# Eight normalised-row buffers shared with the gate tiles, earlier weight halves and a new engine order in a fused attention and feed-forward kernel

## The chip, the cores and the metric

The kernel runs on one core of one Trainium2 chip. The metric is the device time of one execution in microseconds (us). A profiled execution has a span about 2.0 us shorter than its time.

An execution more than 1.5% above the fastest of the same kernel counts as slow and is left out of the ratios.

TensorE is PE, VectorE DVE, ScalarE ACT and GpSimd POOL.

## The reference, cut to what matters

```python
x  = A_x                                   # [1, 2048, 512] bf16
xn = layernorm(x)
q, k, v = split(xn @ wqkv)                 # 32 heads of 16
# each row looks at 8 rows behind it, 2 apart (row, row-2, ... row-14)
logits = einsum(q, k[window]) * scale      # softmax over the 8
s = (softmax(logits) . v[window]) @ wo
h = gelu(xn_in @ w_gate) * (xn_in @ w_up)  # xn_in = xn, 1792 columns
return x + s * silu(h @ w_down)
```

## The kernel before

The 2048 rows are worked on in four blocks of 512, a block being four tiles of 128 rows. Each tile is normalised on DVE into an `xn` buffer and then turned, so that its columns lie along partitions. PE turns the tiles of blocks 0 and 1; a DMA transpose turns those of blocks 2 and 3 (tiles 8 to 15) and frees the `xn` buffer when it has landed. There are four such buffers.

```python
def norm(t, dep):
    def fn():
        tiles["xn", t] = lnpool.tile([P, D], BF16, name="xn_t")    # ring of G["lnb"] = 4
        nc.vector.tensor_scalar(out=tiles["xn", t][:], in0=x_sb[:, t, :], ...)
...
def turned(t, dep):
    def fn():
        nc.sync.dma_start_transpose(out=xnT[:, :, t * P : (t + 1) * P], in_=tiles["xn", t][:])
```

v goes to DRAM and comes back in overlapping windows, by gathers with many short rows. GpSimd and the sync engine issue those of block 0 as soon as v of block 0 is stored, at about 26 us:

```python
def load_values(j, half):
    ...
    a = add("pool", ..., lambda: fn(nc.gpsimd, (0, 1)), deps=[v_stored[j]], ...)
    b = add("sp", 1.0, lambda: fn(nc.sync, (2, 3)), deps=[v_stored[j], ...], ...)
```

The scores of a block are elementwise products of q and shifted k on DVE, pairwise sums (`res`), and a reduction over the head's columns on PE (`L_ps`). Before the first transpose PE runs nine matmuls on zeros, `warm_up(9, TQ)`. A small scheduler in the kernel takes estimated durations (the table `G`) and emits the instructions in the order it finds; on the chip each engine keeps that order.

The softmax here doesn't subtract the row's maximum and nothing guards it: scores larger than these inputs give would overflow.

## Time and profile before

| | kernel before |
|---|---|
| time, three runs | 225.7 us median (225.19 to 225.85) |
| time of the profiled execution | 228.5 us (span 226.6) |
| PE busy | 219.9 us, 97% |
| DVE busy | 185.4 us, 82% |

### The profile page before, as it was taken

How to read it: one execution, taken by the hardware profiler on the slowest of the kernel's cores; microseconds unless marked ns; L12 is line 12 of the kernel's file. 1: busy time of each engine (PE TensorE's matmuls, PEld its weight loads, DVE VectorE, ACT ScalarE, POOL GpSimd, SP SyncE). 2: the span in 40 equal slices, each digit the busy share in tenths (PEclk: the TensorE clock that was granted, in tenths of full speed). 3: DMA queues.
4: the chain of work that ended last, by engine and by line, in shares of the span. 5: the costliest groups of instructions: out<-in, count | busy, mean ns of one | idle time of the engine just before them, and what ended most of it. 6: DMA issues, size and time to landing. Idle time of an engine off the chain costs nothing.

```text
span 226.6 us, 3230 instructions
## 1 busy us (share of the span) xinstructions
PE 219.9 (97%) x1195; PEld 105.4 (47%) x1195; DVE 185.4 (82%) x271; ACT 139.7 (62%) x223; POOL 14.8 (7%) x46
## 2 busy tenths in 40 slices
PE   7999999979999999999999999999999999999994
PEld 2897544534544444444444444444444444444443
DVE  4699979999999999999999989999995997122132
ACT  3368787785778735187986524789735186777211
POOL 7100210000000120000022000002020000000000
PEclk9999999999999999999999999999999999999999
DMA  6935899966960843010062710001662100000001
GB/s 211 360 129 153 205 240 175 227 192 186 337 242 2 188 113 94 30 48 0 3 157 45 175 49 25 23 0 35 157 154 57 48 24 0 0 0 3 23 23 46
DMA packets 23567, 23.68 MB, mean 105 GB/s; under 512 B 5872, under 2 KB 22528, under 8 KB 23552
## 3 DMA queue, kind: packets, MB, share of 16 engines
q1 hardware_dynamic: 17184, 12.75, 22.7%
q10 hardware_dynamic: 5056, 6.46, 9.2%
q0 software_dynamic: 1312, 4.28, 8.3%
q8 instruction: 9, 0.15, 0.3%
q14 instruction: 6, 0.05, 0.1%
HBM read 18.22 MB, written 4.21 MB: 99 GB/s over the span
## 4 chain that ended last, share of the span: by engine, by line
PE 74%; DVE 12%; DMA 5%; ACT 5%; issue 1%; ACTq 0%; DVEq 0%
PE y_ps L818 22%; PE g_ps L756 18%; PE u_ps L756 17%; PE qkv_ps L449 9%; PE s_ps L806 6%; DMA xnT<-xn_t 3%; DVE stats L317 3%; DVE res L561 3%; DVE prod L589 2%; PE O_ps L723 2%; DVE xn_t L338 2%; DMA wo_sb<-in_A_wo_dram 1%; ACT L766 1%; DMA x_sb<-in_A_x_dram 1%; ACT gl L766 1%
## 5 line engine op out<-in xcount | busy, mean ns | idle before, releaser
L756 PE MATMUL g_ps<-xnT,wg_sb 128*128 128x512 bf16 x224 | 57.5, 379 | 0.2
L756 PE MATMUL u_ps<-xnT,wu_sb 128*128 128x512 bf16 x224 | 57.6, 379 | 0.0
L818 PE MATMUL y_ps<-wd_sb,hT 128*128 128x512 bf16 (+2 forms) x238 | 51.5, 367 | 0.0
L449 PE MATMUL qkv_ps<-xnT,wqkv_sb 128*128 128x512 bf16 (+2 forms) x256 | 45.0, 338 | 0.3 <-ACT vst L473 0.2
L766 ACT ACTIVATE gl<-g_ps 128x512 bf16<-128x512 f32 x56 | 33.5, 599 | 11.5 <-PE g_ps L756 10.3
L561 DVE TENSOR_TENSOR res<-prod 128x2048 bf16<-128x2048 bf16 x32 | 39.1, 1221 | 0.5
L777 ACT ACTIVATE hT<-u_ps 128x512 bf16<-128x512 f32 x56 | 33.5, 598 | 9.3 <-PE u_ps L756 9.1
L701 DVE TENSOR_TENSOR prod<-attn,v_arr 128x2048 bf16<-128x2048 bf16 x32 | 38.8, 1219 | 0.0
L589 DVE TENSOR_TENSOR prod<-q_sb,k_sb 128x2048 bf16<-128x2048 bf16 x32 | 38.4, 1218 | 0.0
L818 PEld LDWEIGHTS <-hT 128*128 128x128 bf16 x238 | 22.5, 98 | 26.5 <-issue 1.3
L781 DVE TENSOR_TENSOR hT<-gl,hT 128x512 bf16<-128x512 bf16 x56 | 23.3, 421 | 14.1 <-ACT hT L777 14.0
L449 PEld LDWEIGHTS <-wqkv_sb 128*128 128x128 bf16 x256 | 27.1, 113 | 15.9 <-issue 0.9
L756 PEld LDWEIGHTS <-wg_sb 128*128 128x128 bf16 x224 | 21.7, 98 | 27.4 <-issue 1.9
L756 PEld LDWEIGHTS <-wu_sb 128*128 128x128 bf16 x224 | 21.1, 98 | 26.3 <-issue 2.1
L830 ACT ACTIVATE sil<-y_ps 128x512 bf16<-128x512 f32 (+2 forms) x17 | 9.7, 572 | 34.1 <-PE y_ps L818 34.0
L835 DVE TENSOR_TENSOR sg<-sil,s_ps 128x512 bf16<-128x512 bf16 (+2 forms) x17 | 11.1, 654 | 14.4 <-PE s_ps L806 7.6
L521 POOL DMA_DIRECT2D v_arr<-vT_dram x16 | 9.3, 586 | 150.4 <-DVE prod L701 130.3
L806 PE MATMUL s_ps<-wo_sb,o_sb 128*128 128x512 bf16 (+2 forms) x68 | 16.6, 366 | 0.0
L734 ACT ACTIVATE o_sb<-O_ps 128x1024 bf16<-128x1024 f32 x8 | 8.2, 1023 | 9.0 <-PE O_ps L723 9.0
L462 ACT ACTIVATE q_sb<-qkv_ps 128x512 bf16<-128x512 f32 x16 | 9.6, 599 | 5.5 <-PE qkv_ps L449 5.5
L473 ACT ACTIVATE vst<-qkv_ps 128x512 bf16<-128x512 f32 x16 | 9.1, 597 | 5.7 <-DMA wo_sb<-in_A_wo_dram 2.7
L317 DVE BATCH_NORM_STATS2 stats<-x_sb 128x6 f32<-128x512 bf16 x16 | 10.8, 672 | 2.2 <-DMA x_sb<-in_A_x_dram 2.2
(54 smaller groups left out, 114.7 us busy)
## 6 DMA issues: line engine op xcount, KB each, us to landing
v_arr<-vT_dram POOLq DMA_DIRECT2D x16, 260.0 KB, 5.8
v_arr<-vT_dram SPq DMA_DIRECT2D x16, 260.0 KB, 5.6
vT_dram<-vst SPq DMA_DIRECT2D x16, 128.0 KB, 5.6
out_dram<-sg SPq DMA_DIRECT2D x15, 128.0 KB, 1.7
wu_sb<-in_B_w_up_dram ACTq DMA_DIRECT2D x2, 896.0 KB, 7.1
wg_sb<-in_B_w_gate_dram ACTq DMA_DIRECT2D x2, 896.0 KB, 5.2
wd_sb<-in_B_w_down_dram ACTq DMA_DIRECT2D x1, 1792.0 KB, 11.9
wqkv_sb<-in_A_wqkv_dram SPq DMA_DIRECT2D x2, 512.0 KB, 6.0
```

Of the source, the lines that this page charges most:

```text
L317: nc.vector.bn_stats(out=stats[:, t, :], in_=x_sb[:, t, :])
L449: nc.tensor.matmul(ps[:, i * n : (i + 1) * n], lhsT=wqkv_sb[:, which, ws], rhs=xnT[:, dk, j * TQ + lo : j * TQ + lo + n], start=(dk == 0), ...
L561: nc.vector.tensor_tensor(out=res[:], in0=a[:], in1=b[:], op=ALU.add)
L589: nc.vector.tensor_tensor(out=prod[:], in0=tiles["q", j][:, c, :].unsqueeze(1).to_broadcast([P, 4, TQ]), in1=kwin, op=ALU.mult,)
L701: nc.vector.tensor_tensor(out=prod[:], in0=tiles["attn", j][:, w2, :].unsqueeze(1).to_broadcast([P, 4, TQ]), in1=tiles["va", j, half][:, 4 ...
L756: nc.tensor.matmul(ps[:], lhsT=w[:, dk, fc * P : (fc + 1) * P], rhs=xnT[:, dk, j * TQ : (j + 1) * TQ], start=(dk == 0), stop=(dk == NC - 1),)
L766: nc.scalar.activation(out=tiles["gl", j, fc][:], in_=tiles["g_ps", j, fc][:], func=AF.Gelu_apprx_tanh)
L777: nc.scalar.activation(out=hidden(), in_=tiles["u_ps", j, fc][:], func=AF.Copy)
L781: nc.vector.tensor_tensor(out=h, in0=tiles["gl", j, fc][:], in1=h, op=ALU.mult)
L806: nc.tensor.matmul(tiles["s", t, cs.start][:], lhsT=tiles["o", j][:, c, tt * P : (tt + 1) * P], rhs=wo_sb[:, c, cs], start=(c == 0), stop= ...
L818: nc.tensor.matmul(tiles["y", t, cs.start][:], lhsT=tiles["h", j, fc // (NF // 2)][:, fc % (NF // 2), tt * P : (tt + 1) * P], rhs=wd_sb[:, ...
L835: nc.vector.tensor_tensor(out=tiles["sg", t][:, cs], in0=tiles["sil", t][:, cs], in1=tiles["s", t, cs.start][:], op=ALU.mult,)
```

## The change

The intent is to take the wait for a free `xn` buffer off DVE's way to the first scores. The ring gets eight buffers, and its memory is found by letting the output tiles' silu and gate buffers use the same ring later. The first halves of `w_gate` and `w_up` are loaded earlier, and the order of all engines is found anew from a changed table of durations. Core of the diff, with cuts:

```diff
-    ... xturn=3.702, lnb=4, ... TRACT=((1, 1),), trig=[1, 6, 3, 5], ...
+    ... xturn=4.638, lnb=8, ... TRACT=((1, 1),), trig=[0, 0, 5, 6], ... wd_at=2, ...
...
-    fpool = pool("fpool", 3)
...
-                tiles["xn", t] = lnpool.tile([P, D], BF16, name="xn_t")
+                tiles["xn", t] = lnpool.tile([P, D], BF16, name="xn_t", tag="xn")
...
-                tiles["sil", t] = fpool.tile([P, D], BF16, name="sil")
-                tiles["sg", t] = fpool.tile([P, D], BF16, name="sg")
+                tiles["sil", t] = lnpool.tile([P, D], BF16, name="sil", tag="xn")
+                tiles["sg", t] = lnpool.tile([P, D], BF16, name="sg", tag="xn")
```

(The scheduler's bookkeeping of the ring follows; it is left out here.)

More of the change, by code (lines that the diff above doesn't have):

```diff
@@ L25 @@
 G = dict(
-    MM=0.215, COL8=0.564, COL16=1.157, TR=0.24, PROD=1.197, HMUL2=0.34, STATS=0.766, NORM=0.323,
-    TRCOPY=0.465, ACT1=0.56, ACT2=0.963, TABLE=1.08, HOP=0.248, LOOK=0.046, xturn=3.702, lnb=4,
-    tcol=384, vst=2.785, vload=10.575, vissue=2.707, x2=15.772, x3=17.887, FULL=(0, 1, 2, 3),
-    BETWEEN={1: 6}, NPE=2, TRACT=((1, 1),), trig=[1, 6, 3, 5], s_prio=[1.0, 2.0, 3.5, 4.25],
-    v_prio=[2.0, 2.0, 3.0, 3.5], e_lat=0.796, b_lat=1.188, l_lat=0.1, o_lat=1.013, t_lat=0.381,
-    s_lat=0.105, smode=[2, 2, 2, 0], p_sum=-0.4, p_red=-0.5, p_tr=-1.0, p_h=-1.4, wo_at=0, wd_at=0,
-    fb=4, ab=2, ob=1, prb=3, rsb=4, vab=2, x_early=[3.2, 3.5, 3.8, 4.1],
+    MM=0.214, COL8=0.3, COL16=1.6, TR=0.2, PROD=1.142, HMUL2=0.34, STATS=0.755, NORM=0.328,
+    TRCOPY=0.39, ACT1=0.543, ACT2=0.811, TABLE=1.35, HOP=0.17, LOOK=0, xturn=4.638, lnb=8, tcol=384,
+    vst=2.974, vload=6.199, vissue=3.668, x2=12.258, x3=15.244, FULL=(0, 1, 2, 3), BETWEEN={1: 6},
+    NPE=2, TRACT=((1, 1),), trig=[0, 0, 5, 6], s_prio=[1.0, 3.5, 5.0, 5.0], v_prio=[2.75, 1.75, 3.0,
+    3.0], e_lat=0.291, b_lat=1.428, l_lat=0.468, o_lat=0.81, t_lat=0.496, s_lat=1.042, smode=[2, 2,
+    1, 2], p_sum=-0.4, p_red=-0.5, p_tr=-0.45, p_h=-2.0, wo_at=0, wd_at=2, fb=4, ab=2, ob=1, prb=3,
+    rsb=4, vab=2, x_early=[3.2, 3.5, 3.8, 4.1],
 )
@@ L87, in ready @@
             return None
-        for ring, key in t.takes:
-            n = len(self.taken[ring]) - self.bufs[ring]
+        for i, (ring, key) in enumerate(t.takes):
+            n = len(self.taken[ring]) - self.bufs[ring] + sum(r == ring for r, _ in t.takes[:i])
             if n >= 0:
@@ L185 @@
     order = Order(
-        {"xn": G["lnb"], "q": 3, "vst": 4, "va": G["vab"], "pr": G["prb"], "res": G["rsb"], "attn": 2, "o": 2, "h0": 1, "h1": 1, "gl": 3, "sg": 3,
+        {"xn": G["lnb"], "q": 3, "vst": 4, "va": G["vab"], "pr": G["prb"], "res": G["rsb"], "attn": 2, "o": 2, "h0": 1, "h1": 1, "gl": 3,
          "f": G["fb"], "a": G["ab"], "O": G["ob"]}
@@ L879, in finish @@
                     "act", ACT1, lambda cs=cs: silu(cs), deps=[ym], prio=-0.5, func="silu",
-                    takes=[("sg", t)] if cs.start == 0 else [], frees=[("f", ("y", t, cs.start))],
+                    takes=[("xn", ("sil", t)), ("xn", ("sg", t))] if cs.start == 0 else [], frees=[("f", ("y", t, cs.start))],
                 )
@@ L883, in finish @@
                     "dve", 0.06 + 0.62 * part(cs), lambda cs=cs: gate(cs), deps=[a, sm], prio=-1.8,
-                    frees=[("f", ("s", t, cs.start))],
+                    frees=[("f", ("s", t, cs.start))] + ([("xn", ("sil", t))] if end else []),
                 )
@@ L890, in finish @@
                 st = add("act" if split and end else "sp", 0.6, lambda cs=cs: store(cs), deps=[d], prio=-0.5)
-                add(("dma", "out", t, cs.start), 2.0, lambda: None, deps=[(st, 0.0)], frees=[("sg", t)] if end else [])
+                add(("dma", "out", t, cs.start), 2.0, lambda: None, deps=[(st, 0.0)], frees=[("xn", ("sg", t))] if end else [])
         def in_turn():
```

## The prediction

> **What bounds the kernel now.** I read the page first, then the chain of waits, then the table of who waited for whom, then the timelines of TensorE (PE) and VectorE (DVE). The page gives the engine shares.
>
> ```profile
> span 226.6 us, 3230 instructions
> PE 219.9 (97%) x1195; PEld 105.4 (47%) x1195; DVE 185.4 (82%) x271; ACT 139.7 (62%) x223; POOL 14.8 (7%) x46
> PE 74%; DVE 12%; DMA 5%; ACT 5%; issue 1%; ACTq 0%; DVEq 0%
> ```
>
> PE is the engine that everything ends behind. Busy time alone does not prove it, because matmuls are pipelined and overlap in the record, so I took starts, not durations. In the timeline a group of four 128x512 matmuls starts every 0.86 us (30.91, 31.77, 32.64), that is 216 ns each, and it does so almost without a break from 18.8 us to the last matmul at 223 us. So I looked for every place where the next group starts late. These are the lines, with what stands before and after them.
>
> ```profile
> 45.68 0.40 PE L614 MATMUL L_ps<-res,quad 128*32 128x512 bf16 x4
> 47.36 0.40 PE L614 MATMUL L_ps<-res,quad 128*32 128x512 bf16 x4 [1.28 <-DVE res L561]
> 47.69 5.37 PE L449 MATMUL qkv_ps<-xnT,wqkv_sb 128*128 128x512 bf16 x24
> ...
> 53.22 1.04 PE L449 MATMUL qkv_ps<-xnT,wqkv_sb 128*128 128x512 bf16 x4
> 54.45 1.89 PE L449 MATMUL qkv_ps<-xnT,wqkv_sb 128*128 128x512 bf16 x8 [0.19 <-ACT vst L473]
> ...
> 65.12 0.84 PE L614 MATMUL L_ps<-res,quad 128*32 128x512 bf16 x8
> 65.89 1.04 PE L756 MATMUL g_ps<-xnT,wg_sb 128*128 128x512 bf16 x4
> ...
> 111.04 1.04 PE L756 MATMUL u_ps<-xnT,wu_sb 128*128 128x512 bf16 x4
> 112.19 1.02 PE L756 MATMUL g_ps<-xnT,wg_sb 128*128 128x512 bf16 x4
> ```
>
> The reader should see how little there is. An undisturbed score reduction occupies 0.55 us of PE (the one at 106.71 is followed at 107.26); block 0's takes from 45.68 to 47.69, so 1.46 us are lost. Block 1's takes 0.77, so 0.22 lost. At 53.22 four matmuls should take 0.86 and take 1.23: 0.37 lost. At 111.04 they take 1.15: 0.29 lost, and the same once more at 153.54. Sum: 1.46 + 0.22 + 0.37 + 0.29 + 0.29 = 2.63 us. Outside the start (first transposes at 5.66) and the tail (last matmul at 223.3, end at 226.6), that is all PE waits for.
>
> Where the 1.46 us come from is on DVE, and one step further on the DMA queue:
>
> ```profile
> 31.02 0.41 DVE L338 TENSOR_SCALAR xn_t<-x_sb,mv,rstd 128x512 bf16<-128x512 bf16 x1 [0.26 <-DMA xnT<-xn_t]
> 34.42 0.41 DVE L338 TENSOR_SCALAR xn_t<-x_sb,mv,rstd 128x512 bf16<-128x512 bf16 x1 [1.85 <-DMA xnT<-xn_t]
> 46.08 1.22 DVE L561 TENSOR_TENSOR res<-res 128x2048 bf16<-128x2048 bf16 x1
> ```
>
> Four xn buffers hold the normalised rows until the DMA transpose has read them. The last rows of blocks 2 and 3 wait for that transpose (0.26 + 1.85 = 2.11 us of idle DVE), DVE runs without a pause from there to the res at 46.08, and PE waits for its end at 47.3. One of the transposes landed 7.3 us after its issue; they share those microseconds with w_gate's first half (issued 24.21, landed 29.65) and the first gathers of v.
>
> **What the Trainium skill says.** "TensorE: Matmul & The Clock Gate", section "Back-to-back issue gap", gives N/2.4 + 2.5 ns for a warm matmul, 216 ns at N = 512; this trace has 216. So there is nothing to win inside the matmuls. "Perfetto Trace Analysis", section "Identifying the Most-Contended Engine", warns that matmul busy share is no measure of the roofline; here too the 379 ns mean of a matmul record is far from its 216 ns of spacing, hence my use of starts. "DMA: Bandwidth & Descriptors", section "Issuing engines are not separate DMA queues", says transfers started from different engines share the same 16 DMA engines; the trace agrees: w_down (issued 53.15) took 11.9 us to land and the v stores issued beside it 7.3 to 9.5, against about 2 us alone. "ScalarE: Activation LUTs", section "What ACT_TABLE_LOAD costs", states about 1283 ns a load; the trace has 1283.
>
> **The change part by part.** The number of matmuls on PE is the same and their forms are the same (compared in the instruction order of the built kernel), so only waits and positions can move the time.
>
> Eight xn buffers: all eight normalised tiles of blocks 2 and 3 now stand before the first score product, so the 2.11 us of DVE idle go away. The cost is memory alone, paid by giving the silu and gate tiles the same ring; there are 16 output tiles of two buffers each, so four tiles in flight instead of three. That ring isn't needed by the norms any more when the first output tile comes (about 85 us).
>
> Order at the start: ScalarE (ACT) now does the square root of tile 2 before the first evacuation of q, which removes DVE waits of 0.71 and 0.27 us. But the copy of tile 3 stands behind PE's transpose at about 12.5, with only 1.6 us of statistics to fill the time from 10.2, so about 1.1 us come back as a new DVE wait. Zero in sum. Then I add DVE's start spacings from the trace in the new order: statistics 0.80 a tile, norm 0.33, product 1.14, sum behind its own product 1.25, gate multiply 0.34. From the second pair of norms of block 1 (about 18.2): three tiles of statistics, two pairs of norms, four tiles of statistics, two pairs of norms = 27.1. First half of the scores: 4 products and 3 sums, 8.3 us, 35.4. Second half with six gate multiplies: 10.2 us, 45.6. PE arrives at the reduction's second half at about 46.2. So the 1.46 us go, with about 0.5 us to spare.
>
> From there DVE needs 18.2 us to the end of block 1's scores (47.3 to 65.5 in the trace, with the same list of instructions after the change), so 63.8; PE without its stops needs 17.4, from 46.2 to 63.6. DVE is the bound of this stretch by 0.1 to 0.3 us; of the 0.22 us at block 1 about nothing is saved in itself, but both come 1.6 us earlier.
>
> The 0.37 us at 53.2: ACT issues wo in four pieces and w_down in one, 50.51 to 53.8, before it evacuates v. After the change w_down stands behind block 3's evacuations, 0.6 us fewer here: the stop goes or falls under 0.1.
>
> The exponentials of block 2: today between two gelus, two extra table loads and one of the 0.29 stops. Now behind the last evacuation of block 1's feed-forward, ahead of the silus: PE has 14 matmuls (3.0 us) to run before it needs the result, while ACT needs about 0.7 + 1.28 + 1.02 = 3.0 from PE's start of the reduction, which itself takes 0.55. One 0.29 gone; the one of block 3 keeps its pattern and stays.
>
> New waits: the transposes of tiles 6 and 7 now stand one group of eight matmuls later (19.2), with only 0.88 us of matmuls between them and the first q matmul of block 1, which needs both copies on ACT (two of 0.5 behind a latency of 0.4): about 0.2 us lost.
>
> Weights: first halves issued at 13 instead of 18.6 and 24.2. The second half of w_gate goes from 44.9 to about 56.6; PE needs it at about 66. In that place w_up's half took 9.1 us beside w_down; w_down now comes only at about 64, so 5 to 6 us, landed by 63. w_down itself: 1.8 MB at twice the 4.9 us of a lone 0.9 MB half is under 10 us, landed by 74, needed at about 79. Both fit.
>
> Sum: 1.46 + 0.37 + 0.29 gained = 2.12, less 0.2 (new copy wait), less about 0.2 (DVE-bound stretch to block 1) = 1.7. Adding DVE spacings on through blocks 1 to 3 in the new order, each reduction is ready 0.1 to 1.4 us before PE comes to it, the tightest at the first and last value blocks; I take off another 0.2 for those. Net gain 1.5 us: 225.7 - 1.5 = 224.2.
>
> **The rivals.** First: the score chain stays the bound. My 45.6 for DVE has an error of half a microsecond, and any ACT square root that falls behind an evacuation adds to it. Then the wait at the reduction stays at 0.3 to 0.8 and passes whole into block 1: 225.0 to 225.4. For it: the chain of waits runs through DVE statistics and norms from 12 to 26 us. Second: the early weights steal from x. For it: 1.8 MB are issued while the last x tiles land (13.88). Against: x tile 8 is first read at about 15.7, tile 12 after 22, so 2 us to 8 us of slack. It would make 225.5. Third: a late w_gate half or w_down stops PE for one to three microseconds: 226 to 228. For it: transfers of 9.1 and 11.9 us in this trace; against: they were slow because they ran together, and now don't. Fourth: all waits go, PE runs to its floor: 225.7 - 2.6 = 223.1. Nothing in the profile allows less, since the start and the tail have the same instructions.
>
> **Range and chances.** Between the fourth rival and the first lie 223.1 and 225.4, so 223.0 to 225.5 eight times in ten. Faster by over 2% would need under 221.2, 1.9 us below the floor: 0.02. Slower by over 2% would need a new stop of over 4.5 us, which only the third rival at its worst gives: 0.02.
>
> **What would show it.** Right: no wait of the xn norm for the transpose; PE's reduction of block 0 in under 0.8 us; a stop under 0.1 at the v evacuation; the feed-forward pairs of block 0 resuming at 64.0 to 64.5 instead of 65.89; the last matmul at about 221.8. Wrong: the reduction still waits for res (first rival), a gate or down matmul waits for a weight DMA (third), or new breaks of over 0.3 us at a value reduction.

## The result, and the profile after

| | before | after |
|---|---|---|
| time, four runs each | 225.65 us median (225.19 to 225.85) | 225.03 us median (224.88 to 225.28) |
| ratio of fast runs | | 0.9977, 95% from 0.9959 to 0.9994 |

A ratio here is the mean time of one kernel's fast runs over that of the other's of the same rounds, so not quite the ratio of the medians. The time was in the range. The gain was 0.5 us by the ratio (0.0023 of 225.65), not 1.5.

The page of the changed kernel, shares of the span and the chain that ended last:

```profile
span 222.8 us, 3236 instructions
PE 217.1 (97%) x1195; PEld 103.2 (46%) x1195; DVE 185.2 (83%) x271; ACT 138.9 (62%) x222; POOL 14.8 (7%) x46
PE 68%; DVE 26%; ACT 2%; DMA 1%; issue 1%; DVEq 0%
```

The span is 3.8 us shorter than in the profile before, although the times differ by 0.6 at the median. The DMA share of the chain fell from 5% to 1%, DVE's rose from 12% to 26%. PE's timeline of the changed kernel (start, duration, engine, line, operation, count) shows the places that the prediction named:

```profile
43.86 0.61 PE L613 MATMUL L_ps<-res,quad 128*32 128x512 bf16 x8
44.41 4.51 PE L448 MATMUL qkv_ps<-xnT,wqkv_sb 128*128 128x512 bf16 x20
...
61.49 0.40 PE L613 MATMUL L_ps<-res,quad 128*32 128x512 bf16 x4
62.09 0.40 PE L613 MATMUL L_ps<-res,quad 128*32 128x512 bf16 x4 [0.20 <-DVE res L560]
62.42 1.04 PE L755 MATMUL g_ps<-xnT,wg_sb 128*128 128x512 bf16 x4
...
148.06 1.04 PE L755 MATMUL u_ps<-xnT,wu_sb 128*128 128x512 bf16 x4
149.22 1.02 PE L755 MATMUL g_ps<-xnT,wg_sb 128*128 128x512 bf16 x4
```

Block 0's reduction takes 0.55 us from start to the next start, so nothing is lost there. Block 1's takes 0.93, so 0.37 is lost. At 148.06 four matmuls take 1.16 instead of 0.86; by the starts of the single matmuls 0.28 is lost there. One more stop of 0.24 us lies at 18.39, where q of block 1 waits for the copies of tiles 6 and 7.

So far all of this fits the prediction, and by it the time should have fallen by 1.5 us or more. That it did not pointed to the other side of the comparison, the profile of before.

### The profile page after: what moved, and what is told of

The parts are those of the page before. It is cut to its first block, busy times and chain, and to the rows that moved or that the text cites. A ratio compares the mean times of both kernels' runs of the same rounds, so it can differ in the third digit from the quotient of the medians.

```text
span 222.8 us, 3236 instructions
## 1 busy us (share of the span) xinstructions
PE 217.1 (97%) x1195; PEld 103.2 (46%) x1195; DVE 185.2 (83%) x271; ACT 138.9 (62%) x222; POOL 14.8 (7%) x46
## 4 chain that ended last, share of the span: by engine, by line
PE 68%; DVE 26%; ACT 2%; DMA 1%; issue 1%; DVEq 0%
PE y_ps L817 22%; PE g_ps L755 19%; PE u_ps L755 18%; DVE prod L588 8%; DVE res L560 6%; PE s_ps L805 6%; DVE stats L316 4%; DVE xn_t L337 3%; PE O_ps L722 2%; DVE mv L317 1%; DMA x_sb<-in_A_x_dram 1%; DVE hT L780 1%; DVE xnT L362 1%; ACT L765 1%; ACT gl L765 1%
## 5 line engine op out<-in xcount | busy, mean ns | idle before, releaser
L448 PE MATMUL qkv_ps<-xnT,wqkv_sb 128*128 128x512 bf16 (+2 forms) x256 | 43.3, 326 | 0.1
L448 PEld LDWEIGHTS <-wqkv_sb 128*128 128x128 bf16 x256 | 25.3, 109 | 15.7 <-issue 0.7
```

The costliest lines, as they stand in the source:

```text
L448: nc.tensor.matmul(ps[:, i * n : (i + 1) * n], lhsT=wqkv_sb[:, which, ws], rhs=xnT[:, dk, j * TQ + lo : j * TQ + lo + n], start=(dk == 0), ...
```

## The experiments

Two theories of what the change is worth stand behind the expectations, and some texts call them by letters. The ring theory (R): the four buffers hold DVE back, and the eight buffers take that away. The start theory (S): the profiled execution of before was an unlucky one, whose slow start of PE let the DMA transposes meet the v gathers, and a typical execution has no such wait. Other rivals are named where they stand.

Runs of one job share one chip and the runs of the kernel before. There were three chips: the first four kernels on one, the next eight on a second, the last six on a third.

### 1. The kernel before once more, and the changed one once more

Both unmodified.

> The kernel before, unchanged. In the profiled execution of before, the first 32 matmuls of 128x128 (q of block 0) start every 105 ns; in the profiled execution of the changed kernel every 56 ns, and the span of before's profile (226.6) plus the 2 us that lie between span and time is about 228.5, not the 225.7 of its timed runs. Theory S (the profile of before that I read was an execution with a slow start of TensorE): a new profile has the 56 ns start, a span of 223.5 to 224.0, and the lost time at the reductions L of blocks 0 and 1, the v evacuation and the two exponentials is 1.0 to 1.6 us, not 2.63. Theory N (the start makes no difference, and the changed kernel gives its gain back elsewhere): the span with the 56 ns start is again over 225.5 or the stops again sum to 2.4 us or more. Time against itself: ratio 0.998 to 1.002.

> The changed kernel, unchanged, to have the ratio more closely: 0.996 to 0.998 under S and under N; the profile again with the 56 ns start and a span of 222.7 to 223.3.

Measured: before 225.11 us median (225.03 to 225.25, 4 runs), after 224.88 median (224.87 to 225.48, 6 runs), ratio of after to the before of its rounds 0.9961 (95% from 0.9915 to 1.0006). The second profile of before has span 223.1, 3.5 us less than the first. The start of PE in the first profile, then in the second:

```profile
6.95 5.44 PE L449 MATMUL qkv_ps<-xnT,wqkv_sb 128*128 128x128 bf16 x48
```

```profile
6.79 3.69 PE L449 MATMUL qkv_ps<-xnT,wqkv_sb 128*128 128x128 bf16 x48
```

The same 48 matmuls take 1.75 us more in the first. The first 32 start every 105 ns there and every 56 ns here. "TensorE: Matmul & The Clock Gate", section "What's actually happening", says why this may differ between executions of one kernel: TensorE starts at half its clock and is released by a free-running window of activity of about 3.4 us, so that the number of slow matmuls is "run-variable". This trace's 105 and 56 ns, a factor of 1.9, agree with a half clock; the length of the window isn't read from it.

Later in the second profile of before:

```profile
43.90 0.61 PE L614 MATMUL L_ps<-res,quad 128*32 128x512 bf16 x8
44.45 5.37 PE L449 MATMUL qkv_ps<-xnT,wqkv_sb 128*128 128x512 bf16 x24
...
51.20 1.89 PE L449 MATMUL qkv_ps<-xnT,wqkv_sb 128*128 128x512 bf16 x8 [0.18 <-ACT vst L473]
...
61.87 0.61 PE L614 MATMUL L_ps<-res,quad 128*32 128x512 bf16 x8
62.42 0.82 PE L756 MATMUL g_ps<-xnT,wg_sb 128*128 128x512 bf16 x3
```

Block 0's reduction loses nothing, in the kernel before. No norm waits for a transpose, as DVE's timeline of this profile shows:

```profile
28.73 0.85 DVE L338 TENSOR_SCALAR xn_t<-x_sb,mv,rstd 128x512 bf16<-128x512 bf16 x2
30.71 0.41 DVE L338 TENSOR_SCALAR xn_t<-x_sb,mv,rstd 128x512 bf16<-128x512 bf16 x1
```

The fourth transpose was issued at 25.48, before the first gather of v (26.11), and landed at 30.69, just before the last norm. In the first profile it was issued at 27.09, after the first gather (26.87), and took 7.30 us.

The feed-forward pairs resume at 62.42, to the hundredth where the changed kernel resumes them (its 0.82 and x3 are the edge of the window asked for). The stops of PE, worked out from the starts as in the prediction; the last three columns use the starts of single matmuls, which differ from those of whole groups by up to 0.02:

| lost by PE, us | before, 1st profile | before, 2nd | after, 1st | after, 2nd |
|---|---|---|---|---|
| block 0's reduction | 1.46 | 0 | 0 | 0 |
| block 1's reduction | 0.22 | 0 | 0.37 | 0.29 |
| v evacuation | 0.37 | 0.35 | 0 | 0 |
| exponentials of block 2 | 0.29 | 0.28 | 0 | 0 |
| exponentials of block 3 | 0.29 | 0.28 | 0.28 | 0.28 |
| copies of tiles 6 and 7 | 0 | 0 | 0.24 | 0.24 |
| sum | 2.63 | 0.91 | 0.89 | 0.81 |

An execution of before without the wait has 0.91 us to lose, not 2.63. (The start theory had said 1.0 to 1.6, and a span of 223.5 to 224.0, so both came out a little under it.) The change takes 0.63 of it away and brings 0.53 to 0.61 of new stops. What remains, 0.1 us or less, is smaller than the 0.3 us between the spans (223.1 and 222.8). The rest is won in the start: PE comes to block 0's reduction at 43.90 in the second profile of before and at 43.86 and 43.96 in the changed kernel's two, although the changed kernel has by then lost 0.24 us on the copies. Which part of the new order wins these 0.2 to 0.3 us wasn't tested.

No profile fell on the timed executions of before in the comparison. That they had no such wait is inferred from their times: 225.19 to 225.85, against 225.03 for the profiled execution without it and 228.5 for the one with it.

### 2. Both kernels with a cold TensorE

```diff
-    warm_up(9, TQ)
+    warm_up(0, TQ)
```

> The kernel before without its nine warm-up matmuls, so that TensorE certainly starts slow. Theory S: 228 to 229.5 us (ratio 1.010 to 1.017), the first matmuls at about 105 ns, stops at L of block 0 near those 1.46 us. Theory N: within 0.5 us of before, because VectorE's chain absorbs a slow start.

> The changed kernel without its warm-up matmuls. Theory S: slow start costs it the 1.6 us of the start less the 0.37 us that its reduction of block 1 now waits, so 226.0 to 226.8 us, and the gap to the kernel before with a slow start is 2 to 2.5 us, which is the gain that I predicted before allowances. Theory N: no more than 0.5 us over the changed kernel.

Measured: before 234.22, 229.07, 227.71, 231.61; after 226.18, 226.02, 227.19, 225.89. The cold start costs the changed kernel 1.2 us at the median (226.10 against 224.88). Two of its four (225.89 and 227.19) lie outside the expected 226.0 to 226.8. It costs the kernel before 2.6 us at its fastest (227.71 against 225.11) and 9 at its worst. DVE's timeline of the worst one, which counts as slow and shows the extreme of the wait:

```profile
36.64 0.41 DVE L338 TENSOR_SCALAR xn_t<-x_sb,mv,rstd 128x512 bf16<-128x512 bf16 x1 [6.22 <-DMA xnT<-xn_t]
40.16 0.41 DVE L338 TENSOR_SCALAR xn_t<-x_sb,mv,rstd 128x512 bf16<-128x512 bf16 x1 [1.97 <-DMA xnT<-xn_t]
```

The same wait as in the first profile, four times as long (8.2 us against 2.1). PE's timeline of it shows what else the wait brought:

```profile
44.04 1.86 PE L756 MATMUL g_ps<-xnT,wg_sb 128*128 128x512 bf16 x4 [4.66 <-ACT gl L766]
```

PE stood still for 4.8 us, and after that its granted clock was 0.50 from 44.0 to 47.4 us, so that eight matmuls took 3.37 us instead of 1.73. So a second slow stretch of 1.6 us is part of those 9 us; block 0's reduction lost another 1.05.

Two of the four cold executions of before count as slow. Among the fast ones (229.07 and 227.71) the gap between the cold kernels is 2.3 us at the medians, as the start theory expected (2 to 2.5); over all four it is 4.2.

### 3. One part at a time: the ring, the early weights, the order

The ring alone: the order of every engine is the old one, and only the buffers are eight and shared with the silu and gate tiles (eight plus three separate ones don't fit in memory).

```diff
-    lnpool = pool("lnpool", G["lnb"])
+    lnpool = pool("lnpool", 8)
-                tiles["sil", t] = fpool.tile([P, D], BF16, name="sil")
+                tiles["sil", t] = lnpool.tile([P, D], BF16, name="sil", tag="xn")   # sg likewise
```

> The kernel before with its order untouched on every engine, and only the ring changed: eight xn buffers, shared with the silu and gate tiles. What is known now: the kernel before took 225.0 to 226.3 us in most executions, but 228.4, 228.5 and 233.4 in three, and 227.7 to 234.2 with a slow start, where the xn norms of DVE waited up to 8.2 us for DMA transposes that stood behind the gathers of v. Theory R (the ring): eight buffers take that wait away and nothing else, so the best executions stay at 225.0 to 225.4 and none is over 226.5. Theory O (the new order, or the early weights, is what steadies the kernel): still one execution in eight or so over 227.5.

Measured: 224.95, 225.1, 226.68, 225.61, 224.97, 224.8; median 225.03, ratio 0.9963 (95% from 0.9915 to 1.001). The kernel before took 224.93 to 231.34 beside it (median 226.19 of 11). One execution, 226.68, lies over the 226.5 that the ring theory allowed, and it wasn't profiled. Nothing in the times of the fast executions separates the ring alone from the whole change (best 224.80 against 224.87).

The profile of the ring alone (224.95) has a fast start, and yet its fourth transpose was issued at 25.46, after the first gather (25.31). It took 7.18 us and landed at 32.64. The last norm didn't wait for it:

```profile
30.58 0.40 DVE L337 TENSOR_SCALAR xn_t<-x_sb,mv,rstd 128x512 bf16<-128x512 bf16 x1
```

With four buffers this norm would have had to wait for that landing, an estimated 2.1 us from these two figures. So the ring can take away such a wait in an execution with a fast start too.

The ring alone from a cold start:

> The same, without the warm-up matmuls. Theory R: 226.0 to 227.0 us in all executions, no wait of the xn norm, against 227.7 to 234.2 for the kernel before with a slow start. Theory O: a spread of over 2 us and waits of the norm or a late reduction of block 0.

Measured: 226.67, 225.92, 226.84, 229.05. No norm waits in the profile, though the fourth transpose took 7.4 us there. With four buffers the cold start had given 227.7 to 234.2. The 229.05 was over what the ring theory allowed, and it wasn't profiled.

The early weights alone, from a cold start, all else as before:

```diff
+            if n < 2:   # first halves of w_gate and w_up: issued right behind the copy of tile 2
```

> The kernel before without warm-up matmuls, its order untouched, but the first halves of w_gate and w_up issued by ACT right behind the copy of tile 2 (about 13 us in place of 18 and 24). Theory R: the transposes still stand behind the v gathers, so norm waits of 1 us or more and times spread from 227 to 233. Theory O in its form of early weights: the transposes land within 6 us, no wait over 0.5 us, 226 to 227 in all executions.

Measured: 228.73, 228.03, 228.03, 228.02, all fast. The norm still waits 2.09 us for a transpose that took 6.9 us, and block 0's reduction loses 1.33 us. The loads of weights aren't what holds the transposes up; at most they make the time steadier, but the cold kernel before ran on another chip, so this stays open.

The new order with four buffers:

```diff
-    lnpool = pool("lnpool", G["lnb"])          # 8, in the changed kernel
+    lnpool = pool("lnpool", 4)
+    sgpool = pool("sgpool", 4)                 # for sil and sg
```

> The changed kernel, its order untouched on every engine, but with four xn buffers and a ring of four for silu and gate tiles. Theory R: the norms of tiles 12 to 15, at 23.8 to 25.4 us, wait for the transposes of tiles 8 to 11, which land at 23.9 to 26.9: 2 to 2.5 us of DVE idle, reduction of block 0 late by about 2 us, 226.6 to 227.5 us, more where gathers get in front. Theory O: 224.9 to 225.4 as the changed kernel.

Measured: 229.2, 228.74, 228.87, 228.52, all fast: 3.9 us over the changed kernel on the first chip, more than the ring theory's 1.7 to 2.6. DVE's timeline:

```profile
26.44 0.41 DVE L338 TENSOR_SCALAR xn_t<-x_sb,mv,rstd 128x512 bf16<-128x512 bf16 x1 [1.42 <-DMA xnT<-xn_t]
29.68 0.41 DVE L338 TENSOR_SCALAR xn_t<-x_sb,mv,rstd 128x512 bf16<-128x512 bf16 x1 [2.83 <-DMA xnT<-xn_t]
```

The new order puts all eight norms before the first score product, which only pays with a buffer for each. With four it waits in the profiled execution, where the transposes waited for took 3.2 and 5.2 us, and PE loses 2.74, 1.56 and 0.57 us; the four times agree within 0.7 us, so the others probably waited as well. The old order spreads the last norms between the products, so that four buffers were enough in the second profile of before, where the transposes took 3.3 to 5.7 us. This is why the ring adds so little at the median: the old order had already hidden most of it.

### 4. Are the gathers the cause?

The kernel before from a cold start with four buffers and its order untouched. Only block 0's gathers are held back: a copy of one column, on GpSimd, reads what the fourth DMA transpose writes (tile 11), and all eight gathers stand behind it.

```diff
+        def held():
+            if j == 0 and half == 0:
+                nc.gpsimd.tensor_copy(out=hold[:], in_=xnT[:, 0, 12 * P - 1 : 12 * P])
+            fn(nc.gpsimd, (0, 1, 2, 3) if j == 0 else (0, 1))
```

> The kernel before from a cold TensorE (no warm-up matmuls), 4 xn buffers, every instruction of PE, DVE and ACT in its old place. Only the eight v gathers of block 0, all issued by GpSimd, are held back until the fourth DMA transpose has landed (a one-column copy on GpSimd that reads its result stands in front of them). If the transposes are late because they queue behind these gathers: each of the four transposes lands within 2.5 to 6 us of its issue, no norm waits over 0.3 us for one (the same kernel with the gathers in their old place: 6.22 and 1.97 us), block 0's reduction has no stop of over 0.3 us, and all runs lie between 225.9 and 227.5 (cold start included), none above 228. If the transposes are late for another reason (the weight loads, the v stores, or the cold start itself): waits of 2 to 6 us stay and the runs scatter from 227.7 to 234 as before.

Measured: 226.78, 226.31, 227.54, 226.56 (one 0.04 us over the range). Issue and landing of the first four transposes, from the trace:

| transpose of tile | cold, gathers from 26.41 | took | cold, gathers from 32.09 | took |
|---|---|---|---|---|
| 8 | 21.51 to 24.77 | 3.25 | 21.60 to 25.01 | 3.42 |
| 9 | 24.17 to 29.84 | 5.67 | 24.32 to 29.88 | 5.56 |
| 10 | 25.47 to 36.62 | 11.15 | 25.61 to 30.53 | 4.92 |
| 11 | 26.78 to 40.13 | 13.36 | 26.92 to 30.98 | 4.07 |

The issue times agree within 0.15 us; only the gathers moved. (The first profile is the slow execution of section 2; the fast ones of that kernel took 229.07 and 227.71, on another chip.) The last norms, of tiles 14 and 15, no longer wait, and PE's reduction of block 0 is whole:

```profile
30.10 0.87 DVE L339 TENSOR_SCALAR xn_t<-x_sb,mv,rstd 128x512 bf16<-128x512 bf16 x2
32.02 0.41 DVE L339 TENSOR_SCALAR xn_t<-x_sb,mv,rstd 128x512 bf16<-128x512 bf16 x1
```

```profile
45.44 0.61 PE L620 MATMUL L_ps<-res,quad 128*32 128x512 bf16 x8
45.99 4.29 PE L450 MATMUL qkv_ps<-xnT,wqkv_sb 128*128 128x512 bf16 x19
```

The transposes that now do stand behind the gathers (tiles 14 and 15, issued at 33.25 and 34.56) took 11.3 and 15.6 us, and nobody waited. So it is the gathers, and the wait is theirs to make or leave. One more thing changed with them: the four gathers that the sync engine issued between the transposes are now issued by GpSimd. That alone doesn't help, since the last two transposes were slow behind gathers that all came from GpSimd. Nor does the order of issue alone say how long a transpose takes: in the cold kernel that of tile 10 was issued 0.94 us before the first gather and still took 11.15 us. The same with the nine warm-up matmuls back:

> The same with the nine warm-up matmuls back: the kernel before, 4 xn buffers, its order untouched, block 0's gathers held back. If the gathers are the cause of the tail: 224.9 to 225.5 in every execution, none above 226, with four buffers and without any part of the change; beside it the kernel before itself shows some executions of 226 to 233. If they are not: at least one execution above 226, or a wait of a norm of over 0.3 us in the profile.

Measured: 225.57, 225.42, 225.32, 226.81. Two of four in the expected range, one 0.07 over it, and one over the limit of 226, which by the letter of the expectation speaks against the gathers as the whole cause of the tail. The profile is without a wait of a norm. The fourth was longer by 1.4 us, which is about what a slow start costs; it wasn't profiled, so this stays open.

### 5. The remaining stop at block 1, and the slow starts

DVE bounds the changed kernel up to block 1's reduction. Here ACT copies tiles 4 and 5 in DVE's place, at the same point of the order:

```diff
-                if on_act:
+                if on_act or t in (4, 5):
                     nc.scalar.activation(out=o, in_=i, func=AF.Copy)
```

> The changed kernel with one more thing: the copies of the transposed tiles 4 and 5 out of PSUM are done by ACT instead of DVE, in the same place of the order. DVE is freed of two copies of about 0.4 us ahead of the scores. If DVE is what bounds the stretch up to block 1's reduction: the stop of 0.29 to 0.37 us there goes (under 0.1) and the median is 224.5 to 224.7. Rival: ACT evacuates q and k of block 1 later by the 1.0 us of the two copies, PE waits for a PSUM buffer at 14 to 20 us instead (0.3 us or more), and the time is 224.9 or more.

> The changed kernel once more, on the chip of the run with the copies on ACT, to compare with it. Both theories: 224.8 to 225.0 median, no execution above 225.6, stops of PE 0.24 (copies of tiles 6 and 7), 0.29 to 0.37 (block 1's reduction) and 0.28 (exponentials of block 3).

> The changed kernel with the copies of tiles 4 and 5 on ACT once more, on the chip of the two runs above. If the copies took away the stop at block 1's reduction: 224.4 to 224.7 in executions with a fast start, 226.2 to 226.5 in one with a slow start, and a profile of a fast start shows that reduction without a stop over 0.1 us. If the last run was luck: 224.9 or more.

Measured: with the copies on ACT 226.27, 225.02, 224.57, 224.59, 224.41, 224.7 (median 224.65), and once more, on the third chip, 226.41, 225.18, 226.27, 224.52, 224.63, 224.65 (median 224.91). The changed kernel beside the first: 225.12, 224.89, 226.82, 226.66, 224.92, 226.69 (median 225.89), where no execution above 225.6 had been expected; its profile (225.12) has a stop of 0.17 us at block 1's reduction. The best executions gain about 0.3 us (224.6 against 224.9), though 225.02 and 225.18 fit neither a fast nor a slow start, and both kernels have executions 1.6 to 1.9 us longer. Two of those were profiled, both of the kernel with the copies, and both have the slow start (this is the one of the third chip; the changed kernel took 2.82 for these forty):

```profile
7.04 4.52 PE L448 MATMUL qkv_ps<-xnT,wqkv_sb 128*128 128x128 bf16 x40 [0.16 <-ACT xnT L360]
```

The ring leaves the slow start's own 1.2 to 1.9 us in place. It takes away only what follows from it.

Then eleven warm-up matmuls instead of nine. They end at 5.8 to 6.2 us in the profiles instead of 5.1 to 5.3, so that PE doesn't pause before the first transpose:

```diff
-    warm_up(9, TQ)
+    warm_up(11, TQ)
```

> The kernel before with eleven warm-up matmuls instead of nine, nothing else. They end at about 5.9 instead of 5.1, so that TensorE has no pause of 0.4 us before the first transpose at 5.7. If the slow starts (q matmuls of block 0 every 105 ns instead of 56, as in the profile that the prediction rests on) come from that pause, and if a slow start is what pushes an execution into the transposes' wait: 225.1 to 225.7 in every execution, none above 226, while the kernel before beside it shows some of 226 to 233. If the transposes meet the gathers by other chance too: the q matmuls are all at 56 ns but executions of 226 to 231 remain. If the pause has nothing to do with the slow start: the spread is that of the kernel before, and the median is up to 0.3 us later.

> The changed kernel with the copies of tiles 4 and 5 on ACT and eleven warm-up matmuls. If the pause causes the slow starts: 224.4 to 224.9 in every execution, none of 226.3 to 226.8. If not: some executions of 226.2 to 226.8 remain, as in the last two runs of the changed kernel.

> The kernel before with eleven warm-up matmuls once more, for the count. If the slow start is the trigger of the tail and the longer warm-up prevents it: at most one execution of six above 226, none above 227, while the kernel before beside it has some above 227 (10 of 34 so far). If the last six were luck: two or more above 227.

> The changed kernel with two copies on ACT and eleven warm-up matmuls once more, for the count. If the longer warm-up prevents slow starts: all six between 224.4 and 225.2. If the last six were luck: one or two at 226.2 to 226.8, as 6 of the 28 executions with nine warm-up matmuls.

> The changed kernel with eleven warm-up matmuls and nothing else. If the longer warm-up prevents slow starts: all six between 224.8 and 225.5, median 224.9 to 225.1 (the copies' gain of 0.2 to 0.3 is absent). If not: some at 226.6 to 226.8.

| eleven warm-up matmuls | runs, us |
|---|---|
| before | 224.88, 225.19, 224.86, 225.31, 225.32, 226.53 |
| before, again | 225.34, 225.47, 225.52, 227.61, 226.55, 227.02 |
| after | 225.23, 224.86, 225.24, 225.32, 224.96, 225.1 |
| after, copies on ACT | 224.72, 224.85, 224.75, 224.82, 224.47, 224.87 |
| after, copies on ACT, again | 225.06, 224.85, 224.5, 225.01, 224.58, 224.39 |

With the whole change, 18 of 18 executions lie at 225.32 or below; with nine matmuls 6 of 28 were at 226.27 or above. By chance alone 18 in a row would come about once in 77 times (22/28 to the 18th power), if all chips had one rate. They may not: on the third chip, where all 18 ran, only six ran with nine matmuls, two of them long. "TensorE: Matmul & The Clock Gate", section "Why this matters for your kernels", asks for 4 us of matmuls to be past the slow clock; nine of 427 ns are 3.8 us. The runs agree with it; whether it is the missing pause or the two more matmuls that counts wasn't separated. PE of the changed kernel with both edits:

```profile
1.27 4.84 PE L299 MATMUL warm_ps<-warm 128*128 128x512 bf16 x11 [1.27 <-DVE eps_sb L239]
5.94 0.73 PE L352 MATMUL tr_ps<-ident,xn_t 128*128 128x128 bf16 x8
7.02 2.82 PE L448 MATMUL qkv_ps<-xnT,wqkv_sb 128*128 128x128 bf16 x40 [0.35 <-ACT xnT L360]
...
61.87 0.61 PE L613 MATMUL L_ps<-res,quad 128*32 128x512 bf16 x8
62.42 1.04 PE L755 MATMUL g_ps<-xnT,wg_sb 128*128 128x512 bf16 x4
```

The forty q matmuls run fast, and block 1's reduction is whole. This version has the lowest times: median 224.79 and 224.72, and its worst of twelve is 225.06. Its ratios to before, 0.9952 (0.9897 to 1.0006) and 0.9951 (0.9901 to 1.0001), have intervals that just reach 1. Its margin over the changed kernel with the same warm-up, 225.17, is about 0.4 us. The stop at block 1 alone doesn't account for that: in the profile of the latter (225.23) it was only 0.10 us, and the q matmuls began at 7.26 instead of 7.02.

The kernel before kept a tail with eleven matmuls: 4 of 12 at 226.5 to 227.6, none of 228 or more. The first six fitted the theory that the slow start is the trigger of the tail but for one, the second six did not. So the slow start is probably not the only way in. No profile fell on one of those executions, and what tips them over stays open; the ring alone (section 3) shows one way that needs no slow start, a first gather issued 0.15 us ahead of the fourth transpose.

## Why the prediction was wrong

**The first term of the sum, 1.46 us, is the step that failed.** It read block 0's lost time in one profile and subtracted it from the median of other executions. The second profile of before has 0 in its place. The wait behind it, 2.11 us of DVE for the transposes, was real and rightly traced to the transposes sharing their time with v's gathers (section 4 shows it by moving only the gathers), but it belongs to some executions. The sign was there: that execution took 228.5 us against a median of 225.7.

**With 0 in place of 1.46 the sum comes close to the measurement, and a little under it.** The other gains (0.37 and 0.29) measured 0.35 and 0.28. The new copy wait, put at 0.2, measured 0.24. The DVE-bound stretch to block 1, put at 0.2, measured 0.29 to 0.37. That leaves 0.63 - 0.53 to 0.61, about 0.1 or less, where the timed gain is 0.2 to 0.6 (225.11 to 224.88; 225.65 to 225.03). The prediction had put the new order at the start at zero in sum; there 0.2 to 0.3 us were won (section 1).

**One sum is not complete as written.** The DVE spacings named up to 27.1 add up to 26.4. The missing 0.7 are the four reciprocals between them, about 0.17 each; with them the sum was right, since that stretch took 9.0 us in the changed kernel (16.32 to 25.35), against 8.9.

**The rivals.** Weights were no trouble: w_gate's second half, issued at 54.70, landed at 60.00 (63 was allowed), and w_down at 69.56 (74 allowed). The first halves landed at 16.9 and 19.6, later than a lone load would, without a wait. The rival of a score chain that stays the bound came true in a small way: a wait of 0.29 to 0.37 us appeared at block 1. Its time, 225.0 to 225.4, holds the measured 225.03, but by luck: it had 0.3 to 0.8 us of block 0's wait staying, and that was 0 in both kernels. None of the rivals was the right one, that the wait isn't there to begin with.

**The signs that were to show it right appeared, but for two times, and proved little.** No wait of the norm, a reduction of 0.55 us, no stop at the v evacuation: the first two hold in the second profile of the unchanged kernel as well. The pairs were to resume at 64.0 to 64.5 and the last matmul to come at 221.8; they came at 62.42 and 219.6 (the end of the last, as the prediction counted it), early by the slow start that the second execution didn't have, which the prediction had taken as fixed.

**What the change is worth.** Over all executions beside the experiments, slow ones too, before took over 227 us in 10 of 35 and up to 233.44 (mean 226.6, median 225.78). The changed kernel took at most 226.82 in 16 (mean 225.3, median 224.98). The two sets aren't from the same chips in equal parts. The gain lies mainly in the tail, and the ratio of fast runs, by its rule, shows little of it.

## What to carry to other kernels

Compare the time of the profiled execution with the median before you add up its waits. If it is longer, profile again, and count only the waits that both profiles have. A wait for a transfer can be a matter of what else was issued in the same microsecond; to find out, delay the other transfer behind a real dependence and leave everything else in its place. A deeper ring may be worth nothing at the median and much in the tail, and a new order may then depend on it.

## What the Trainium skill lacked or had wrong

- "DMA: Bandwidth & Descriptors", section "DMA Transpose (X-bar)", says nothing of how long a transpose takes beside other transfers. Here one of 128x512 bf16 took 2.3 us at the fastest (the changed kernel), 2.9 to 5.6 us where it landed ahead of the held-back gathers (section 4), and up to 16.4 us behind them (the kernel before with late gathers).
- No page read for this case says that such a wait can come and go between executions of one kernel on one chip: 224.93 to 231.34 us for the kernel before on the second chip.
- "TensorE: Matmul & The Clock Gate" puts the cost of the slow start under 1% of a span. By itself it was that here (1.2 to 1.9 us of 225), but it can push other work into a wait: from a cold start the kernel before, with four buffers, took 2.6 and 4.0 us more in its fast executions, and 9.1 in the worst, where the wait brought a second slow stretch.
